# A global-filter token mixer and a hard-swish FFN on one core: the 3008-point Fourier transform factored as 47 x 64 in the other order, with token blocks cut across 94-token units

## The chip, the cores and the metric

One core of one Trainium2 chip. The metric is device microseconds of one execution. Runs of one kernel agree here within about 0.2%. A ratio is the mean time of one kernel's runs over that of the kernel before's runs of the same rounds on the same chip, so it is not quite the ratio of the medians that are quoted beside it.

## The reference

```python
# x: (8, 3008, 256); filt_r, filt_i: (1505, 256); w_in: (256, 2048); w_out: (2048, 256); x and filters float32, w_in and w_out float64
X = np.fft.rfft(x, axis=1)
Y = X * (filt_r + 1j * filt_i)[None, :, :]
y = np.fft.irfft(Y, n=3008, axis=1).reshape(8 * 3008, 256)
h = y @ w_in
out = (h * np.clip(h + 3.0, 0.0, 6.0) / 6.0) @ w_out          # (24064, 256)
```

## The kernel before

3008 = 47 x 64. Each batch's transform runs in two stages of dense matrices with a pass through memory between them, is multiplied by the filter, and comes back in two stages. In the kernel before, the first stage takes 64-point transforms over 47 residues (groups of four residues in two halves: 6 units a batch, four 64x64 matmuls of 512 columns each). The second stage has 32 matrices of 96 x 128, the inverse second stage 32 of 128 x 96; two matrices make a unit. The last inverse stage (`n_unit`) puts 4 x 128 tokens into a block of 512. The FFN takes 47 blocks in 8 steps each (376 steps), with Strassen products: 7 matmuls of 256 columns and 14 of 128 columns a step. Batch 0 is transformed ahead of the loop; batches 1 to 7 are transformed between the FFN steps of earlier batches.

```python
def b_unit(b, i):                                   # second stage, two matrices
    ...
    for u in range(2):
        nc.tensor.matmul(ps[:, u, :], st["tab", b, c][0][:, r + u, :],
                         st["t2", b, c][:, r + u, :], start=True, stop=True)

def bi_unit(b, i):                                  # its inverse
    ...
    for u in range(2):
        nc.tensor.matmul(ps[0:KR, u, :], st["tab", b, c][1][:, r + u, :], y[:, u, :], start=True, stop=True)

def n_unit(k, dh):                                  # last inverse stage: half of a block of 512 tokens
    ...
    for q in range(XC):                             # XC = 4
        nc.tensor.matmul(ps[:, ts(q, P)], st["t4", k][:, q, ts(dh, P)], wai, start=True, stop=True)

def out_5(k):                                       # the last sum of a block and its stores
    ...
    for q, n, _, ends in runs(k):
        for h, (b, n1) in enumerate(ends):
            nc.gpsimd.dma_start(rows[b, :, n1:n1 + n, :], o[h * 64:h * 64 + 64, q:q + n, :])

# ... batch 0, ahead of the loop; convert() makes float32 of one of 16 parts of the float64 FFN weights, on VectorE and GpSimd
for c in range(NB):                                 # NB = 6
    a_unit(0, c)
    z_store(0, c, nc.scalar)
    ...
    if c < 4:
        convert(1)
for i in range(K2 // 2 + 1):                        # 16 units of the second stage and its inverse
    ...
    if i % 4 == 2:
        convert(1)
```

In a matmul here the second operand is stationary (its weights are loaded) and the third is streamed. In `n_unit` the stationary operand is the data, 128 channels wide, and the streamed one is the table `wai`, one column a token.

## Time and profile before

| | before |
|---|---|
| median of the rounds shared with the changed kernel | 2854.55 us |
| span of the profiled run, mean granted clock | 2851.6 us, 0.986 |
| TensorE, VectorE, ScalarE, GpSimd busy | 96%, 74%, 47%, 18% |
| batch 0 done, loop begins (end of the first `psn` group on the chain) | 155.5 us |
| last matmul ends, span ends | 2842.1, 2851.6 us |

The stretches, and what binds each, are worked out in the prediction.

Names in the views: `psf` takes the results of the first, second and inverse second stage, `psn` those of the last inverse stage, `al` and `be` those of the FFN's up projection, `po` those of its down projection. An fp32 matmul stands in the trace as two records. The granted clock is the share of full speed that the throttle gave TensorE. "HWDGE" in the prediction means the DMAs that SP and ACT issue (the page calls their queues hardware_dynamic).

The end of the kernel before, in order of time (start, us, engine, line, operation):

```profile
2844.36 2.12 POOL L500 DMA_DIRECT2D out_dram<-o  x4 [0.51 <-POOL o L492]
```

Four stores, each from 64 partitions and 512 rows of output in all, are issued within 2.12 us, and 9.5 us after the last matmul the kernel is over.

### The profile page before, as it was taken

The numbers are of one execution on the slowest core, as the hardware profiler recorded it, in microseconds if no ns is written. First come the engines' busy times: TensorE is split into PE (matmuls) and PEld (weight loads), VectorE is DVE, ScalarE is ACT, GpSimd is POOL, SyncE is SP. The second block draws the span as 40 slices with busy tenths as digits, with TensorE's granted clock in tenths as the row PEclk, the third lists the DMA queues.
The fourth block names the chain that finished last, engine by engine and source line by source line (L and its number), as shares of the span: only waits on it lengthen the run. The fifth ranks groups of instructions, "written<-read, shape, count | busy, mean of one in ns | idle before, by whom it ended". The sixth has DMA issues, their size and how long they took to land.

```text
span 2851.6 us, 46327 instructions
## 1 busy us (share of the span) xinstructions
PE 2732.0 (96%) x17952; PEld 2469.6 (87%) x17952; DVE 2108.7 (74%) x3663; ACT 1326.1 (47%) x2622; POOL 520.3 (18%) x855
## 2 busy tenths in 40 slices
PE   3669999999999999999999999999999999999998
PEld 1347889999999999999999999999999999999998
DVE  4877877777767777777777777777777777766666
ACT  1124444544454445444544544454445444454544
POOL 2364221211121112111211121112110110010000
PEclk9779999999999999999999999999999999999999
DMA  7464533232222223222331332223221211010000
GB/s 190 137 162 132 152 107 90 72 86 78 71 78 81 79 72 84 70 78 79 87 96 47 93 85 64 83 60 95 77 63 54 71 51 54 17 51 16 23 8 16
DMA packets 104510, 221.66 MB, mean 78 GB/s; under 512 B 19936, under 2 KB 56932, under 8 KB 104292
## 3 DMA queue, kind: packets, MB, share of 16 engines
q1 hardware_dynamic: 69732, 127.97, 16.2%
q0 software_dynamic: 29056, 84.44, 10.5%
q10 hardware_dynamic: 5504, 6.30, 0.7%
q8 instruction: 142, 2.33, 0.4%
q14 instruction: 76, 0.62, 0.1%
HBM read 139.46 MB, written 79.17 MB: 77 GB/s over the span
## 4 chain that ended last, share of the span: by engine, by line
PE 91%; DVE 4%; DMA 3%; issue 1%; ACT 1%; SPq 0%; ACTq 0%; POOL 0%; POOLq 0%; DVEq 0%
PE po L465 40%; PE al L389 22%; PE be L389 17%; PE psf L301 4%; PE psf L329 4%; PE psn L374 3%; PE psf L275 2%; DMA z_tmp<-t 1%; DVE g L439 0%; DMA g_tmp<-t 0%; DVE s L315 0%; DVE s L314 0%; DMA ft<-in_filt_i_dram 0%; DMA ft<-in_filt_r_dram 0%; DVE rest L219 0%
## 5 line engine op out<-in xcount | busy, mean ns | idle before, releaser
L465 PEld LDWEIGHTS po<-w_out,g 128*128 128x128 f32 x10528 | 1409.6, 192 | 136.6 <-DVE g L439 25.0
L465 PE MATMUL po<-w_out,g 128*128 128x128 f32 x10528 | 1428.3, 276 | 24.3 <-DVE g L439 23.2
L434 ACT ACTIVATE r<-h,half_c 128x512 f32<-128x512 f32 x752 | 542.5, 721 | 331.6 <-DVE h L415 319.2
L389 PE MATMUL al<-xt,w_in 128*128 128x256 f32 x2256 | 676.7, 382 | 1.3 <-DVE h L420 0.8
L439 DVE SCALAR_TENSOR_TENSOR g<-r,h 128x512 f32<-128x512 f32 x752 | 517.5, 688 | 189.7 <-ACT r L434 173.7
L389 PE MATMUL be<-xn,w_in 128*128 128x256 f32 x1504 | 447.9, 379 | 0.0
L415 DVE TENSOR_TENSOR h<-be,s 128x512 f32<-128x512 f32 x376 | 259.8, 691 | 245.0 <-PE be L389 223.3
L389 PEld LDWEIGHTS al<-xt,w_in 128*128 128x128 f32 x2256 | 343.7, 193 | 3.3 <-issue 1.9
L429 ACT ACTIVATE h<-al 128x256 f32<-128x256 f32 x376 | 144.1, 383 | 383.6 <-PE al L389 383.6
L389 PEld LDWEIGHTS be<-xn,w_in 128*128 128x128 f32 x1504 | 286.0, 190 | 39.1 <-ACT xn L376 0.2
L420 DVE TENSOR_TENSOR h<-al,s 128x256 f32<-128x256 f32 x376 | 159.5, 424 | 199.5 <-PE al L389 199.4
L447 DVE TENSOR_TENSOR g<-g 128x512 f32<-128x512 f32 x376 | 261.6, 696 | 12.9
L410 ACT ACTIVATE s<-al 128x256 f32<-128x256 f32 x376 | 144.1, 383 | 222.3 <-PE al L389 222.3
L289 POOL DMA_DIRECT2D z_tmp<-t x336 | 166.5, 502 | 441.7 <-ACT t L278 426.3
L401 ACT ACTIVATE s<-be 128x256 f32<-128x256 f32 x376 | 144.1, 383 | 181.4 <-PE be L389 181.4
L389 PE MATMUL al<-xn,w_in 128*128 128x256 f32 x752 | 225.0, 381 | 0.5 <-ACT h L429 0.5
L389 PE MATMUL be<-xt,w_in 128*128 128x256 f32 x752 | 224.1, 380 | 0.0
L400 ACT ACTIVATE s<-al 128x256 f32<-128x256 f32 x376 | 144.1, 383 | 70.4 <-PE al L389 70.4
L449 DVE TENSOR_TENSOR g<-g 128x256 f32<-128x256 f32 x376 | 164.2, 437 | 12.8
L446 DVE TENSOR_TENSOR g<-g 128x256 f32<-128x256 f32 x376 | 164.1, 436 | 12.8
L301 PE MATMUL psf<-t,wb 96*128 96x256 f32 x512 | 143.2, 405 | 28.2 <-DMA t<-z_tmp 18.4
L382 POOL TENSOR_TENSOR xt<-xn 128x256 f32<-128x256 f32 x94 | 72.9, 776 | 521.0 <-ACT xn L376 520.9
(52 smaller groups left out, 2011.1 us busy)
## 6 DMA issues: line engine op xcount, KB each, us to landing
ft<-f_tmp SPq DMA_DIRECT2D x48, 512.0 KB
xc<-in_x_dram SPq DMA_DIRECT2D x88, 256.0 KB
z_tmp<-t POOLq DMA_DIRECT2D x336, 64.0 KB, 2.0
t<-z_tmp SPq DMA_DIRECT2D x56, 384.0 KB
g_tmp<-t POOLq DMA_DIRECT2D x56, 384.0 KB, 4.8
t<-g_tmp SPq DMA_DIRECT2D x160, 128.0 KB
out_dram<-o POOLq DMA_DIRECT2D x80, 256.0 KB, 3.7
wb<-wb_t SPq DMA_DIRECT2D x64, 192.0 KB
```

Source lines behind the costliest of these rows:

```text
L289: q.dma_start(z_d[b, :, r0 + h * H:r0 + h * H + 2, :], t[p0:p0 + 32, h, :, :])
L301: nc.tensor.matmul(ps[:, u, :], st["tab", b, c][0][:, r + u, :], st["t2", b, c][:, r + u, :], start=True, stop=True)
L389: nc.tensor.matmul(ps, w_in[p][:, w, :], x, start=start, stop=stop, skip_group_check=True)
L400: nc.scalar.activation(out=s[:, 0, :], in_=al, func=AXT.Copy)
L415: nc.vector.tensor_tensor(out=st["h"][0].rearrange("p (a n) -> p a n", a=2), in0=be, in1=s, op=ALU.add)
L420: nc.vector.tensor_tensor(out=st["h"][1][:, 256:512], in0=al, in1=s5, op=ALU.add)
L434: nc.scalar.activation(out=r, in_=st["h"][i], func=AXT.Relu, bias=half_c, scale=1.0 / 6.0)
L439: nc.vector.scalar_tensor_tensor(out=st["g", k, p][:, o:o + 2, :].rearrange("p a n -> p (a n)"), in0=st["r", i], scalar=1.0, in1=st["h"][i ...
L446: v.tensor_tensor(out=g[:, G1, :], in0=g[:, G3, :], in1=g[:, G22, :], op=ALU.add)
L447: v.tensor_tensor(out=g[:, G3:G2 + 1:2, :], in0=g[:, G3:G1 + 1, :], in1=g[:, G11:G11 + 1, :].broadcast_to([P, 2, 256]), op=ALU.subtract)
L449: v.tensor_tensor(out=g[:, G4, :], in0=g[:, G12, :], in1=g[:, G2, :], op=ALU.subtract)
L465: nc.tensor.matmul(st["po", k][bank][:, part, u, :], g[:, a, ts(u, P)], w_out[p][:, w, :], start=(p == 0 and n in OPENS and u == 0), stop= ...
```

## The change

The factors swap places. The 47-point stage comes first (with 24 of its 47 frequencies, as the input is real), in 8 units a batch in place of 6. The second stage then has 24 full matrices of 128 x 128 in place of 32 of 96 x 128, and so has its inverse. The last inverse stage gives units of 94 tokens, so that a block of 512 tokens is made of 6 or 7 pieces of units. The filter can be read straight from its tensor, and the stores move from GpSimd to SP, cut at unit and tile edges. The intent is a quarter less work in the second stages, on TensorE and on VectorE.

```diff
-N1 = 47        H = 24        K2 = 32        KR = 96      # (constants gathered on one line here)
+NA = 47        NC = 64       KH = 24        TOK = 94     # NB = 8 units, NU = 12 units of two matrices
...
-            nc.tensor.matmul(ps[0:KR, u, :], st["tab", b, c][1][:, r + u, :], y[:, u, :], start=True, stop=True)
+            nc.tensor.matmul(ps[:, u, :], st["tab", b, c][1][:, r + u, :], y[:, u, :], start=True, stop=True)
...
+    def pieces(k):
+        t = k * BLK
+        while t < (k + 1) * BLK:
+            u, r = divmod(t, TOK)
+            n = min(TOK - r, (k + 1) * BLK - t)
+            yield u // HC, u % HC, r, n, t - k * BLK
+            t += n
...
-        for q in range(XC):
-            nc.tensor.matmul(ps[:, ts(q, P)], st["t4", k][:, q, ts(dh, P)], wai, start=True, stop=True)
+        for i, (_, _, r, n, o) in enumerate(pieces(k)):
+            nc.tensor.matmul(ps[:, ds(o, n)], t4[k % 2][:, i, ts(dh, P)], wai[:, ds(r, n)], start=True, stop=True)
...
-        for q, n, _, ends in runs(k):
-            for h, (b, n1) in enumerate(ends):
-                nc.gpsimd.dma_start(rows[b, :, n1:n1 + n, :], o[h * 64:h * 64 + 64, q:q + n, :])
+        for b, j, r, n, t in pieces(k):
+            while n:
+                h, a = divmod(r, NA)
+                m = min(NA - a, n, P - t % P)
+                nc.sync.dma_start(raw(out, b * N + a * NC + h * HC + j, [[NC * D, m], [1, D]]),
+                                  o[t % P:t % P + m, t // P, :])
+                r, t, n = r + m, t + m, n - m
```

(Cut: the tables, the loads and stores between the stages, the places of the units among the FFN steps, and the scratch tiles of the weight conversions, which now share buffers with the filter units.)

More of the change, by code (lines that the diff above doesn't have):

```diff
@@ L21 @@
 N = 3008
-N1 = 47
-N2 = 64
+NA = 47
+NC = 64
+KH = 24
 NF = N // 2 + 1
@@ L28 @@
 DFF = 2048
-JT = DFF // P
-H = 24
-K2 = 32
-SL = 48
-KR = 2 * SL
 HALF = 64
+HC = NC // 2
 XC = 4
-NB = H // XC
+NB = HC // XC
 TC = 4
-NT = K2 // TC
+NT = KH // TC
+TB = 3
+NU = KH // 2
 NP = DFF // 256
-TB = 3
+TOK = 2 * NA
+BLK = 512
+NBLK = B * N // BLK
 def _make_tables():
-    n2 = np.arange(N2)
+    a = np.arange(NA)
+    c = np.arange(NC)
     wa = np.zeros((P, P))
-    wai = np.zeros((P, P))
+    wai = np.zeros((P, TOK))
     for h in range(2):
-        r = slice(h * 64, h * 64 + 64)
-        for k2 in range(K2):
-            th = 2 * np.pi * ((n2 * k2) % N2) / N2
-            c, s = np.cos(th), np.sin(th)
-            wa[r, k2] = wa[r, 64 + k2] = c
-            wai[h * 64 + k2, r] = c * (2.0 if k2 else 1.0)
-            if k2:
-                wa[r, 32 + k2] = wa[r, 96 + k2] = -s
-                wai[h * 64 + 32 + k2, r] = -2.0 * s
-            else:
-                alt = 1.0 - 2.0 * (n2 % 2)
-                wa[r, 32] = wa[r, 96] = alt
-                wai[h * 64 + 32, r] = alt
-    n1 = np.arange(N1)
-    wb = np.zeros((KR, K2, P))
-    wi = np.zeros((P, K2, KR))
-    re, im = slice(0, N1), slice(SL, SL + N1)
-    for k2 in range(K2):
-        for s in range(2 * H):
-            if s < H:
-                k, sign, q = k2 + 64 * s, 1.0, s
-            else:
-                j = s - H + 1
-                k, sign, q = 64 * j - (k2 if k2 else 32), -1.0, 32 + s - H
-                if j == H and k2:
-                    continue
-            th = 2 * np.pi * ((n1 * k) % N) / N
-            c, sn = np.cos(th), np.sin(th)
-            if k in (0, NF - 1):
-                sn = np.zeros(N1)
-            yr, yi = np.zeros(KR), np.zeros(KR)
-            if k2:
-                wb[re, k2, q] = c
-                wb[im, k2, q] = sign * sn
-                wb[re, k2, HALF + q] = -sn
-                wb[im, k2, HALF + q] = sign * c
-                yr[re], yr[im] = c, sign * sn
-                yi[re], yi[im] = -sn, sign * c
-            else:
-                rows = re if s < H else im
-                wb[rows, k2, q] = c
-                wb[rows, k2, HALF + q] = -sn
-                m = 1.0 if k in (0, NF - 1) else 2.0
-                yr[rows], yi[rows] = m * c, -m * sn
-            wi[q, k2], wi[HALF + q, k2] = yr, yi
@@ new lines, in _make_tables @@
+        for k in range(KH):
+            th = 2 * np.pi * ((a * k) % NA) / NA
+            for g in range(2):
+                wa[h * 64:h * 64 + NA, g * 64 + k] = np.cos(th)
+                wa[h * 64:h * 64 + NA, g * 64 + 32 + k] = -np.sin(th)
+            m = 2.0 if k else 1.0
+            wai[h * 64 + k, h * NA:(h + 1) * NA] = m * np.cos(th)
+            wai[h * 64 + 32 + k, h * NA:(h + 1) * NA] = -m * np.sin(th)
+    wb = np.zeros((P, KH, P))
+    wi = np.zeros((P, KH, P))
+    re, im = slice(0, NC), slice(NC, P)
@@ new lines, in _make_tables @@
+    for k in range(KH):
+        for q in range(64):
+            f, sign = (k + NA * q, 1.0) if q < 32 else (NA * (q - 31) - k, -1.0)
+            th = 2 * np.pi * ((c * f) % N) / N
+            cs, sn = np.cos(th), np.sin(th)
+            if f in (0, NF - 1):
+                sn = np.zeros(NC)
+            wb[re, k, q], wb[im, k, q] = cs, sign * sn
+            wb[re, k, HALF + q], wb[im, k, HALF + q] = -sn, sign * cs
+            wi[q, k, re], wi[q, k, im] = cs, sign * sn
+            wi[HALF + q, k, re], wi[HALF + q, k, im] = -sn, sign * cs
@@ L114 @@
     wi_d = nc.inline_tensor(wi_np, name="wi_t").ap()
-    z_d = nc.dram_tensor("z_tmp", (B, K2, KR, D), FP32, kind="Internal").ap()
-    g_d = nc.dram_tensor("g_tmp", (B, K2, KR, D), FP32, kind="Internal").ap()
-    f_d = nc.dram_tensor("f_tmp", (NT, P, TC, D), FP32, kind="Internal").ap()
+    z_d = nc.dram_tensor("z_tmp", (B, KH, P, D), FP32, kind="Internal").ap()
+    g_d = nc.dram_tensor("g_tmp", (B, KH, P, D), FP32, kind="Internal").ap()
     def pool(name, bufs, **kw):
@@ L124 @@
     const = pool("const", 1)
-    xp = pool("xp", 3)
     t1p = pool("t1p", 2)
@@ L131 @@
     t3p = pool("t3p", 2)
-    t4p = pool("t4p", 2)
     xnp = pool("xnp", 2)
@@ L138 @@
     op = pool("op", 2)
-    cv = pool("cv", 4)
     psF = pool("psF", 2, space=PSUM)
@@ L144 @@
     wa = const.tile([P, P], FP32, name="wa")
-    wai = const.tile([P, P], FP32, name="wai")
-    ft = [const.tile([P, TC, D], FP32, name="ft%d" % c) for c in range(TB)]
+    wai = const.tile([P, TOK], FP32, name="wai")
+    xs = [const.tile([P, XC, D], FP32, name="xs%d" % i) for i in range(3)]
+    ft = [const.tile([P, TC, D], FP32, name="ft%d" % i) for i in range(TB)]
+    t4 = [const.tile([P, 7, D], FP32, name="t4%d" % i) for i in range(2)]
     w_in = [const.tile([P, 7, P], FP32, name="w_in%d" % p) for p in range(NP)]
@@ L154, in raw, with table_load @@
         return bass.AP(tensor=src.tensor, offset=src.offset + row * D, ap=ap)
-    def f_load(b, c):
+    def table_load(b, c):
         t = ft[(b * NT + c) % TB]
-        if b > 1:
-            nc.sync.dma_start(t, f_d[c])
-            return
-        lo = 1 if c == 0 else 0
         for src, p0 in ((filt_r, 0), (filt_i, HALF)):
-            for r, n in ((0, 16), (16, H - 16)):
-                nc.sync.dma_start(t[p0 + r:p0 + r + n, :, :].rearrange("p a d -> p (a d)"),
-                                  raw(src, c * TC + 64 * r, [[64 * D, n], [1, TC * D]]))
-                if c == 0:
-                    nc.sync.dma_start(t[p0 + 32 + r:p0 + 32 + r + n, 0, :],
-                                      raw(src, 32 + 64 * r, [[64 * D, n], [1, D]]))
-                n = min(n, H - 1 - r)
-                nc.sync.dma_start(t[p0 + 32 + r:p0 + 32 + r + n, lo:TC, :],
-                                  raw(src, 64 + 64 * r - c * TC - lo, [[64 * D, n], [-D, TC - lo], [1, D]]))
-    def table_load(b, c):
-        f_load(b, c)
-        wb = tabp.tile([KR, TC, P], FP32, name="wb")
+            nc.sync.dma_start(t[p0:p0 + 32, :, :].rearrange("p k d -> p (k d)"),
+                              raw(src, c * TC, [[NA * D, 32], [1, TC * D]]))
+            nc.sync.dma_start(t[p0 + 32:p0 + 64, :, :], raw(src, NA - c * TC, [[NA * D, 32], [-D, TC], [1, D]]))
+        wb = tabp.tile([P, TC, P], FP32, name="wb")
         nc.sync.dma_start(wb, wb_d[:, ts(c, TC), :])
-        wi = tabp.tile([P, TC, KR], FP32, name="wi")
+        wi = tabp.tile([P, TC, P], FP32, name="wi")
         nc.sync.dma_start(wi, wi_d[:, ts(c, TC), :])
         st["tab", b, c] = wb, wi
-        if b == 1:
-            nc.gpsimd.dma_start(f_d[c], ft[(b * NT + c) % TB])
     NCONV = 16
@@ L213, in w_conv @@
         lo, hi = words[:, :, 0], words[:, :, 1]
-        big = cv.tile([P, 512], I32, name="big", tag="cv")
-        rest = cv.tile([P, 512], I32, name="rest", tag="cv")
+        big, rest = (sp.tile([P, 2, D], FP32, name=s).bitcast(I32).rearrange("p a n -> p (a n)")
+                     for s in ("s1", "s2"))
         v = nc.vector
@@ L256, in x_load @@
     def x_load(b, c):
-        t = xp.tile([P, XC, D], FP32, name="xc")
-        if c == NB - 1:
-            nc.vector.memset(t[64:P, XC - 1, :], 0.0)
-        rows = x[b].rearrange("(n2 n1) d -> n2 n1 d", n1=N1)
+        t = xs[(b * NB + c) % 3]
+        rows = x[b].rearrange("(a c) d -> a c d", c=NC)
         for h in range(2):
-            lo = h * H + c * XC
-            w = min(XC, N1 - lo)
-            nc.sync.dma_start(t[h * 64:h * 64 + 64, 0:w, :], rows[:, lo:lo + w, :])
-        st["x", b, c] = t
+            for r, n in ((0, 32), (32, NA - 32)):
+                nc.sync.dma_start(t[h * 64 + r:h * 64 + r + n, :, :], rows[r:r + n, ds(h * HC + c * XC, XC), :])
     def a_unit(b, c):
-        xc = st.pop(("x", b, c))
+        xc = xs[(b * NB + c) % 3]
         t = t1p.tile([P, 2, XC // 2, D], FP32, name="t1")
@@ L286, in z_store @@
                 p0 = g * 64 + ri * 32
-                r0 = ri * SL + c * XC + 2 * g
+                z = z_d[b, :, ts(ri, NC), :].rearrange("k (h j) d -> k h j d", h=2)
                 for h in range(2):
-                    q.dma_start(z_d[b, :, r0 + h * H:r0 + h * H + 2, :], t[p0:p0 + 32, h, :, :])
+                    q.dma_start(z[:, h, ds(c * XC + 2 * g, 2), :], t[p0:p0 + KH, h, :, :])
     def t2_load(b, c, q=None):
         q = q or nc.sync
-        t = t2p.tile([KR, TC, D], FP32, name="t2")
+        t = t2p.tile([P, TC, D], FP32, name="t2")
         q.dma_start(t, z_d[b, ts(c, TC), :, :].rearrange("k p d -> p k d"))
@@ L328, in bi_unit @@
         for u in range(2):
-            nc.tensor.matmul(ps[0:KR, u, :], st["tab", b, c][1][:, r + u, :], y[:, u, :], start=True, stop=True)
+            nc.tensor.matmul(ps[:, u, :], st["tab", b, c][1][:, r + u, :], y[:, u, :], start=True, stop=True)
         if r == 0:
-            st["t3", b, c] = t3p.tile([KR, TC, D], FP32, name="t3")
-        nc.scalar.activation(out=st["t3", b, c][:, r:r + 2, :], in_=ps[0:KR], func=AXT.Copy)
+            st["t3", b, c] = t3p.tile([P, TC, D], FP32, name="t3")
+        nc.scalar.activation(out=st["t3", b, c][:, r:r + 2, :], in_=ps, func=AXT.Copy)
     def g_store(b, c, q=None):
@@ L336, in g_store, with t4_load @@
         q.dma_start(g_d[b, ts(c, TC), :, :].rearrange("k p d -> p k d"), st.pop(("t3", b, c)))
-    def parts(k):
-        for q in range(XC):
-            v, j = divmod(XC * k + q, N1)
-            if j == N1 - 1:
-                yield q, 1, ((2 * v, H - 1), (2 * v + 1, H - 1))
-            else:
-                b, i = 2 * v + j // (H - 1), j % (H - 1)
-                yield q, 0, ((b, i), (b, H + i))
-    def runs(k):
-        found = []
-        for q, kind, ends in parts(k):
-            if found and not kind and not found[-1][2] and found[-1][3][0][0] == ends[0][0]:
-                found[-1][1] += 1
-            else:
-                found.append([q, 1, kind, ends])
-        return found
-    def t4_load(k):
-        t = t4p.tile([P, XC, D], FP32, name="t4")
-        for q, n, _, ends in runs(k):
-            for h, (b, n1) in enumerate(ends):
+    def pieces(k):
[5 more added lines that the diff above has]
+            t += n
+    def t4_load(k):
+        slot = 0
+        found = []
+        for b, j, _, _, _ in pieces(k):
+            if found and found[-1][0] == b:
+                found[-1][2] += 1
+            else:
+                found.append([b, j, 1])
+        for b, j, n in found:
+            for h in range(2):
                 for ri in range(2):
                     p0 = h * 64 + ri * 32
-                    nc.sync.dma_start(t[p0:p0 + 32, q:q + n, :],
-                                      g_d[b, :, ri * SL + n1:ri * SL + n1 + n, :])
-        st["t4", k] = t
+                    nc.sync.dma_start(t4[k % 2][p0:p0 + KH, slot:slot + n, :],
+                                      g_d[b, :, ds(ri * NC + h * HC + j, n), :])
+            slot += n
     def n_unit(k, dh):
@@ L372, in n_unit @@
         ps = psF.tile([P, 512], FP32, name="psn", tag="f")
-        for q in range(XC):
-            nc.tensor.matmul(ps[:, ts(q, P)], st["t4", k][:, q, ts(dh, P)], wai, start=True, stop=True)
+        for i, (_, _, r, n, o) in enumerate(pieces(k)):
+            nc.tensor.matmul(ps[:, ds(o, n)], t4[k % 2][:, i, ts(dh, P)], wai[:, ds(r, n)], start=True, stop=True)
         x = st["xn", k]
@@ L496, in out_5 @@
         o = st.pop(("o", k))[0].rearrange("p t u d -> p (t u) d")
-        rows = out.rearrange("(b n2 n1) d -> b n2 n1 d", n1=N1, n2=N2)
-        for q, n, _, ends in runs(k):
-            for h, (b, n1) in enumerate(ends):
-                nc.gpsimd.dma_start(rows[b, :, n1:n1 + n, :], o[h * 64:h * 64 + 64, q:q + n, :])
-    NBLK = B * N // 512
-    first = [(N1 * (b // 2) + (H - 1) * (b % 2)) // XC for b in range(B)]
+        for b, j, r, n, t in pieces(k):
[5 more added lines that the diff above has]
+                r, t, n = r + m, t + m, n - m
+    first = [b * N // BLK for b in range(B)]
     plan = {}
@@ L516 @@
         nc.vector.memset(half_c, 0.5)
+        for t in xs:
+            nc.gpsimd.memset(t, 0.0)
         nc.sync.dma_start(wa, wa_d)
@@ L521 @@
         w_load(1)
-        for t in ft:
-            nc.vector.memset(t, 0.0)
         done = 0
@@ L543 @@
         nc.sync.dma_start(wai, wai_d)
-        for i in range(K2 // 2 + 1):
-            if i < K2 // 2:
+        for t in t4:
+            nc.gpsimd.memset(t, 0.0)
+        for i in range(NU + 1):
+            if i < NU:
                 b_unit(0, i)
@@ L584, in places @@
             k = first[n]
-            u = [K2 // 2 - 1 - i for i in range(K2 // 2)]
+            u = [NU - 1 - i for i in range(NU)]
             b_at = [(k - 2 - j // 3) * NP + 6 - 2 * (j % 3) for j in u]
             bi_at = [i + 3 for i in b_at]
-            a_at = [(k - 13 + c) * NP for c in range(NB)]
+            a_at = [(k - 7 + c // 4) * NP + (0, 2, 5, 7)[c % 4] for c in range(NB)]
             if n == 1:
                 a_at = list(range(NB))
-                b_at = [8 + 3 * i // 2 for i in range(K2 // 2)]
-                bi_at = [10 + (3 * i + 1) // 2 for i in range(K2 // 2)]
-            elif n == 2:
-                a_at = [10 + 3 * c for c in range(NB)]
+                b_at = [10 + 7 * i // 4 for i in range(NU)]
+                bi_at = [i + 3 for i in b_at]
             return a_at, b_at, bi_at
@@ L605 @@
                 elif n > 1:
-                    at(max(prev[0][c + 3], s - 6), x_load, n, c)
+                    at(max(prev[0][c + NB - 3], s - 6), x_load, n, c)
             for c in range(NT):
-                s = bi_at[2 * (c - TB) + 1] if c >= TB else a_at[-1] + 2
+                s = bi_at[2 * (c - TB) + 1] if c >= TB else a_at[-1] + 1
                 if n > 1 and c < TB:
@@ L612 @@
                 at(s, t2_load, n, c)
-            for i in range(K2 // 2):
+            for i in range(NU):
                 at(b_at[i], b_unit, n, i)
```

## The prediction

> **What bounds the kernel now.** I read the page first, then the busy times by stretch, then the chain of waits. Section 1 of the page names the candidate:
>
> ```profile
> PE 2732.0 (96%) x17952; PEld 2469.6 (87%) x17952; DVE 2108.7 (74%) x3663; ACT 1326.1 (47%) x2622; POOL 520.3 (18%) x855
> ```
>
> A 96% average can hide stages, so I asked for four stretches (first the transform of batch 0, then the start of the block loop, the loop, the end; columns: PE, weight loads, DVE, ACT, POOL, clock, DMA share, GB/s):
>
> ```profile
> 0.00:155.00 155.00, 74.70 (x191) 38.83 (x192) 97.14 (x157) 17.87 (x30) 42.48 (x63) 0.86 0.61 166
> 155.00:240.00 85.00, 60.80 (x323) 46.77 (x323) 72.63 (x118) 27.46 (x55) 65.29 (x101) 0.84 0.48 123
> 240.00:2845.00 2605.00, 2596.47 (x17442) 2384.00 (x17440) 1938.97 (x3389) 1280.81 (x2537) 411.01 (x691) 1.00 0.25 71
> ```
>
> From 240 us on, TensorE is busy 2596.47 of 2605 us: it is the bound, and any matmul removed or added there moves the end. Before that it is not: 0 to 155 us goes through loads, the store of the first stage and VectorE. The chain of waits shows what each piece costs on the path in the loop (start, us, instructions; one fp32 matmul is two records):
>
> ```profile
> 1396.03 0.86 PE be L389 x4
> 1396.89 0.86 PE psf L301 x4
> ...
> 1403.04 0.86 PE be L389 x4
> 1403.90 0.86 PE psf L329 x4
> 1404.77 0.44 PE po L465 x4
> ...
> 1410.05 0.86 PE be L389 x4
> 1410.92 1.02 PE psf L275 x8
> 1411.94 0.64 PE po L465 x4
> ```
>
> The reader is to see: two second-stage matmuls of 256 columns take 0.86 us, so 0.43 each; a first-stage unit takes 1.02 and delays what follows by 0.64 - 0.45 = 0.19, so 1.21; two 128-column matmuls take 0.44, so 0.22 each. An FFN step alone takes 7.01 - 0.86 = 6.15 us.
>
> **What the Trainium skill says.** (1) "TensorE: Matmul & The Clock Gate", section "LDWEIGHTS (loading the stationary operand)": a load takes P/1.2 ns, P the columns of the stationary operand, 107 ns at 128, however few columns are streamed. The trace agrees in slope:
>
> ```profile
> L275 PEld LDWEIGHTS psf<-xc,wa 64*64 64x64 f32 x384 | 13.7, 141 | 52.9 <-ACT t L278 25.0 <-issue 18.0 <-DVE s L315 3.7
> L374 PEld LDWEIGHTS psn<-wai,t 128*128 128x128 f32 x752 | 100.1, 194 | 13.5 <-issue 8.8
> ```
>
> 64 columns more cost 194 - 141 = 53 ns (0.83 ns a column); the other 88 ns are latency, overlapped, since loads follow each other every 110 ns. (2) The same page, "Back-to-back issue gap": N/2.4 + 2.5 ns per pass when warm, and the spacing of a load-and-matmul stream is set by both. In an fp32 record two passes of 128 columns should take 106.7 ns plus about 5; 110 is measured, so a 128-column matmul already stands at its weight load. (3) "TensorEngine Tiling (Array Packing)", "Tiling Modes": 64x64 gives four independent tiles. Agrees: four 512-column matmuls in 1.02 us, where one alone would need 0.86. (4) "DMA: Bandwidth & Descriptors", section "Why a DMA increments its semaphore by 16 and not by 1": the number of engines is the largest divisor up to 16 of the slowest dimension, and on HWDGE the lowest-numbered engines. The kernel before stores 64 rows at a time, so no line of its trace tests this.
>
> **The change part by part.** Counts are of the two built programs.
>
> Second stage and its inverse: 256 + 256 matmuls become 192 + 192. An eighth belongs to batch 0, ahead of the loop. In the loop 448 become 336: -112 x 0.43 = **-48 us**. That the matrices grow from 96 to 128 rows costs nothing in streamed columns.
>
> First stage: 48 units become 64, in the loop 42 become 56: +14 x 1.21 = **+17 us**.
>
> Last inverse stage (psn): here the hidden cost lies. The moved columns stay at 48,128 in all, but a block of 512 tokens now takes 6 or 7 pieces of at most 94 columns in place of 4 of 128, so 376 matmuls become 604. A 94-column record streams 2 x 94/2.4 = 78 ns, less than its 107 ns weight load (the stationary side is the 128-column data tile). If the load sets the pace each piece costs the same 0.22 us as a full one: in the loop 592 - 368 = 224 more, **+49.5 us**. FFN products and sums are untouched. TensorE's sum in the loop: -48 + 17 + 49.5 = **+18 us**; the saving is paid back.
>
> VectorE: two matmuls share a unit of five operations of 0.69 us, and 128 units become 96: -110 us, of which 7/8 lie beside a full TensorE and count for nothing. In batch 0, VectorE does bind: the chain of waits puts four units and one weight conversion at about 20.7 us (81.9 to 102.6 to 123.3). Twelve units and three conversions in place of sixteen and four: **-21 us**. The conversion left over goes to the loop's start, where VectorE is the limit: +5 at most, I take +3.
>
> Start: eight first-stage units in place of six. A unit takes 6.6 us here, set by the store of z_tmp (evictions at 10.3, 17.6, 23.3, 29.6, 35.7, 43.2). The bytes are the same, but 64 DMAs go out in place of 48, from 24 rows. Between +0 and +13; I take **+8**. So the loop starts at about 155 - 13 = 142 us.
>
> End: the page shows stores that go out from GpSimd in pieces of 256 KB:
>
> ```profile
> out_dram<-o POOLq DMA_DIRECT2D x80, 256.0 KB, 3.7
> q10 hardware_dynamic: 5504, 6.30, 0.7%
> ```
>
> The new stores are 696 DMAs on SP, cut at 47-row and 128-row edges. Walking the pieces with rule (4), 18,376 of 24,064 rows fall to a single engine (47 rows: 1 engine), 356 to 435 in each block, 359 in the last. The ACT queue's packets, of 1.1 KB, took 0.7% x 16 x 2851.6 / 5504 = 58 ns each; so a block's store holds one engine for some 23 us of its 57 us, and the last one for 21. Before, TensorE ends at 2842.1 and the span 9.5 us later. After, I estimate 1.7 (last sums) + 1 + 21 + 2 = 26: **+16 us**.
>
> Sum: 2854 + 18 - 13 + 3 + 16 = 2878; plus 6 for new waits where batches meet (below): **2884 us**.
>
> **The rivals.**
> (a) The weight load does not set the pace of short matmuls. Then psn costs nothing more beyond a few ns a piece (some 228 x 15 = 3 us), TensorE's loop falls by about 28 us, and the time is near 2838. For it: loads can run ahead, and PEld is busy 87% with overlapping records. Against it: the slope above, and a load of 107 ns per 78 ns of streaming can't be hidden in a row of such pieces; only the first one of six or seven.
> (b) The queue of one DMA engine becomes a wait. With 23 us of stores and its 1/16 of the rest (183 MB/16 = 11.5 MB at some 58 ns a KB: 670 us in the span, 14 us a block), the engine is about 65% full: no bound by itself, but loads issued behind a block's store wait up to 23 us. Most loads are issued 7 to 10 steps of 6.15 us ahead. The tight ones are the first inverse load of each batch, issued three steps (18 us) before its use and two steps after a store burst, and the second stage's first load, now two to three steps behind the last first-stage unit. Seven such meetings of 0 to 7 us: 6 is my guess for the sum, 50 the worst. If a 1-row packet costs 120 ns in place of 58, the engine is overfull, and stores and loads drag the loop to 3000 or more.
> (c) GpSimd is freed of 112 stores and gains 112 of z_tmp: no change; at 18% busy it binds nothing.
> (d) The end's store is spread over all engines after all: then 16 us less, 2868.
>
> **Range and chances.** (a) at its fullest and a short end give 2825; the sum without guesses gives 2878; bad queueing at every meeting gives 2930. I hold the weight-load argument at 85%, and one-engine stores at 80%. Eight times in ten: 2848 to 2920. The edges of 2% are 2797 and 2911: below needs a gain that no part of the sum holds (0.04); above needs (b) to bite (0.18).
>
> **What would show it.** Right: the psn group has 1208 records, and seven pieces take 1.5 us on the chain of waits with records 110 ns apart even for 94 columns; second-stage groups have 384 records each at 0.43 us a matmul on the path; the loop begins near 142 us; TensorE still about full after 240 us; the span ends some 26 us after the last matmul. Wrong: psn pieces that follow at 80 ns a record (rival a); idle TensorE before psn or second-stage matmuls put down to a DMA (rival b); a tail under 15 us (d). What would upset the number most is a slow single-engine store, which I could not see in the trace before.

## The result, and the profile after

The changed kernel takes 2875.36 us (median of 4 runs, 2874.12 to 2877.08) against 2854.55; the ratio is 1.0072 (95% interval 1.0055 to 1.009). It computes the right result. By the 2% rule it is the same; it is slower by 0.7%, clear of noise. The prediction said 2884.

| | before | after | predicted |
|---|---|---|---|
| first second-stage matmul of batch 0 | 57.3 us | 61.2 us | +8 |
| from there to the first `psn` | 94.6 us | 74.5 us | -21 |
| loop begins | 155.5 us | 141.0 us | 142 |
| loop, to the last matmul | 2686.6 us | 2710.6 us (+24) | +27 (18 of work, 3, 6) |
| last matmul to end | 9.5 us | 20.7 us (+11) | +16 |

The page's first section, and the stretches of the changed kernel (columns as in the prediction):

```profile
PE 2745.6 (96%) x18280; PEld 2487.8 (87%) x18280; DVE 1991.8 (69%) x3492; ACT 1326.2 (46%) x2622; POOL 508.7 (18%) x836
```

```profile
0.00:141.00 141.00, 65.72 (x185) 33.07 (x186) 75.68 (x124) 17.73 (x30) 42.96 (x60) 0.86 0.60 182
141.00:230.00 89.00, 62.68 (x319) 46.84 (x319) 76.68 (x123) 26.50 (x53) 69.14 (x101) 0.84 0.39 110
...
500.00:1000.00 500.00, 500.00 (x3398) 459.87 (x3397) 352.97 (x621) 244.55 (x484) 79.88 (x138) 1.00 0.28 80
```

The table is of one profile of each kernel. Five other profiles of the changed kernel's start, from experiments below that alter nothing before the loop, have the first second-stage matmul at 62.9 to 66.4 us in place of 61.2; from there to the first `psn` they take 74.8 to 77.6 us, so their loop begins 2 to 7 us later. The first row is thus +4 here and +6 to +9 there; of the kernel before there is one profile.

VectorE lost 117 us of work, as meant, and TensorE stayed the bound: 500 of 500 us busy. So those 117 us bought time only ahead of the loop. The chain of waits of the changed kernel shows a half block's seven pieces, and the groups show what they are (out x in, count, then busy us and mean ns):

```profile
1417.21 0.86 PE be L341 x4
1418.08 1.48 PE psn L326 x14
1419.55 0.53 PE po L417 x4
```

```profile
L326 PEld LDWEIGHTS psn<-wai,t 128*128 128x128 f32 x1208 | 152.0, 194 | 15.3 <-issue 10.6
L326 PE MATMUL psn<-wai,t 128*128 128x94 f32 x840 | 115.0, 283 | 9.7 <-DMA t<-g_tmp 9.7
```

Seven matmuls of at most 94 columns take 1.48 us, and the pair after them 0.53 in place of 0.45: 1.56 / 7 = 0.223 us each, though 94 columns at the rate of a 256-column matmul (0.43 us) would stream in 0.158. Records of the down projection that have run tell how far each kernel is (x is their count; each step has 28). Before, then after:

```profile
0.00:500.00 500.00, 154.80 (x1092) 0.93 0.50 138
0.00:1000.00 1000.00, 420.32 (x3056) 0.96 0.39 108
...
0.00:2500.00 2500.00, 1223.85 (x9008) 0.99 0.31 86
```

```profile
0.00:500.00 500.00, 165.54 (x1160) 0.93 0.40 116
0.00:1000.00 1000.00, 431.60 (x3123) 0.97 0.34 98
...
0.00:2500.00 2500.00, 1227.12 (x8992) 0.99 0.29 83
```

At 500 us the changed kernel is 68 records ahead (17 us at some 4 records a us), at 1000 still 67, and at 2500 it is 16 behind. The shorter start is given back in the full loop. No wait takes part in that: of TensorE's waits from 230 us on the longest and the only one for a transfer are

```profile
PE po L417 <- DVE g L391: 1.5, 2, 0.9
...
PE psn L326 <- DMA t<-g_tmp: 0.4, 1, 0.4
```

(us in total, times, longest). Last, the end: the last sum and the stores in order of time, then three stretches after it (last column GB/s):

```profile
2852.90 0.43 DVE L447 TENSOR_TENSOR o<-po,o 128x256 f32<-128x256 f32 x1
2853.36 10.49 SPq L453 DMA_DIRECT2D out_dram<-o  x14
```

```profile
2858.00:2864.00 6.00, 0.00 (x0) 0.00 (x0) 0.00 (x0) 0.00 (x0) 0.00 (x0) 0.50 0.10 31
2864.00:2870.00 6.00, 0.00 (x0) 0.00 (x0) 0.00 (x0) 0.00 (x0) 0.00 (x0) 0.50 0.07 24
2870.00:2872.00 2.00, 0.00 (x0) 0.00 (x0) 0.00 (x0) 0.00 (x0) 0.00 (x0) 0.50 0.02 8
```

Fourteen stores are issued in 10.49 us, and for six more microseconds data goes out at 24 GB/s with a DMA share of 0.07, about 1 of 16 engines.

### The profile page after: what moved, and what is told of

Its sections match the earlier page's. It is cut to its first block, busy times and chain, and to the rows that moved or that the text cites. A ratio compares the mean times of both kernels' runs of the same rounds, so it can differ in the third digit from the quotient of the medians.

```text
span 2872.3 us, 47938 instructions
## 1 busy us (share of the span) xinstructions
PE 2745.6 (96%) x18280; PEld 2487.8 (87%) x18280; DVE 1991.8 (69%) x3492; ACT 1326.2 (46%) x2622; POOL 508.7 (18%) x836
## 4 chain that ended last, share of the span: by engine, by line
PE 90%; DVE 4%; DMA 3%; POOL 1%; issue 1%; SPq 1%; ACT 1%; ACTq 0%; POOLq 0%; DVEq 0%
PE po L417 40%; PE al L341 22%; PE be L341 16%; PE psn L326 4%; PE psf L257 3%; PE psf L285 3%; PE psf L231 2%; DMA z_tmp<-t 1%; SPq L453 0%; DVE g L391 0%; DVE s L271 0%; DMA out_dram<-o 0%; DVE s L270 0%; POOL z_tmp L245 0%; DMA bits<-in_moe_w_out_dram 0%
## 5 line engine op out<-in xcount | busy, mean ns | idle before, releaser
L245 POOL DMA_DIRECT2D z_tmp<-t x448 | 226.2, 513 | 375.5 <-ACT t L234 366.9
L326 PEld LDWEIGHTS psn<-wai,t 128*128 128x128 f32 x1208 | 152.0, 194 | 15.3 <-issue 10.6
L341 PEld LDWEIGHTS be<-xt,w_in 128*128 128x128 f32 x752 | 143.2, 190 | 19.4
```

Source lines behind the costliest of these rows:

```text
L245: q.dma_start(z[:, h, ds(c * XC + 2 * g, 2), :], t[p0:p0 + KH, h, :, :])
L326: nc.tensor.matmul(ps[:, ds(o, n)], t4[k % 2][:, i, ts(dh, P)], wai[:, ds(r, n)], start=True, stop=True)
L341: nc.tensor.matmul(ps, w_in[p][:, w, :], x, start=start, stop=stop, skip_group_check=True)
```

## The experiments

My theory: a short fp32 matmul costs its weight loads and not its columns, so the last inverse stage took back the second stages' saving; the start gained on VectorE; and the end waits for one DMA engine. The rivals are in the expectations. Each edit is made on the changed kernel unless it says otherwise.

**Every piece cut in two** (right result).

```diff
-            nc.tensor.matmul(ps[:, ds(o, n)], t4[k % 2][:, i, ts(dh, P)], wai[:, ds(r, n)], start=True, stop=True)
+            for r2, n2, o2 in ((r, n // 2, o), (r + n // 2, n - n // 2, o + n // 2)):
+                nc.tensor.matmul(ps[:, ds(o2, n2)], t4[k % 2][:, i, ts(dh, P)], wai[:, ds(r2, n2)], start=True, stop=True)
```

> The changed kernel with every piece of the last inverse stage cut in two: 1208 matmuls in place of 604, the same columns streamed, correct result. Theory (a short fp32 matmul costs its two weight loads, 0.22 us, whatever it streams): 592 more in the loop x 0.222 = +131 us, so about 3006 us, and the chain of waits shows 13 or so pieces in some 2.9 us with records 110 ns apart. Rival (cost follows the columns, plus a few ns a matmul): under +10 us, so about 2883.

Measured: 3026.8 us, ratio 1.0599 (1.0583 to 1.0615); about +151 us. The chain of waits of this run:

```profile
1430.98 2.60 PE psn L327 x24
1433.58 0.52 PE po L418 x4
```

Twelve matmuls of 47 columns and fewer take 2.60 + 0.07 us: 0.223 each, the same as at 94 columns. The rival is out by an order of size. Most of the 20 us above the expected 131 go with a lower clock: the mean granted clock was 0.978 over 3026.2 us against 0.985 over 2872.3, and scaled to full clock the two spans would differ by 2959.6 - 2829.2 = 130 us, a rough figure, as the start waits for transfers and VectorE. In the trace the clock falls to one half nine times between 416 and 2813 us, for 3.4 us each, which costs some 15 us; in the changed kernel it stays full from 213 to 2855 us. Whether the rows of short matmuls bring this on, no run tests.

**Four full matmuls in place of the pieces** (wrong result; every load kept).

```diff
-        for i, (_, _, r, n, o) in enumerate(pieces(k)):
-            nc.tensor.matmul(ps[:, ds(o, n)], t4[k % 2][:, i, ts(dh, P)], wai[:, ds(r, n)], start=True, stop=True)
+        for q in range(4):
+            nc.tensor.matmul(ps[:, ts(q, P)], t4[k % 2][:, q, ts(dh, P)], wai, start=True, stop=True)
```

(`wai` is widened to 128 columns.)

> The changed kernel with four 128-column matmuls for each half of a block in the last inverse stage, as the kernel before had, in place of six or seven pieces; wrong result on purpose (the columns belong to the wrong units), all loads kept. Same columns, 376 matmuls in place of 604. Theory (weight load sets the pace): 224 fewer in the loop x 0.222 = -50 us, about 2826 us. Rival (cost follows the columns): no change, 2872 to 2876.

Measured: 2827.02 us, ratio 0.9900 (0.9885 to 0.9915), against 1.0072 for the changed kernel: -0.0172 x 2855 = -49 us. Each ratio is known to some 4 to 5 us; the term of +49.5 us in the prediction agrees within that. Without it the change would have gained 1%.

**The same pieces, but each streams up to 128 columns** (what is too much is overwritten by the next piece).

```diff
-            nc.tensor.matmul(ps[:, ds(o, n)], t4[k % 2][:, i, ts(dh, P)], wai[:, ds(r, n)], start=True, stop=True)
+            w = min(P, BLK - o)
+            nc.tensor.matmul(ps[:, ds(o, w)], t4[k % 2][:, i, ts(dh, P)], wai[:, ds(r, w)], start=True, stop=True)
```

(`wai` is repeated to 256 columns.)

> The changed kernel with the pieces of the last inverse stage streaming up to 128 columns each (what is too much is overwritten by the next piece, so the result is right): 604 matmuls as before, 21,120 more columns streamed, which is 35 us[...]. Theory (up to 128 columns the weight load sets the pace): no change, within 3 us of 2875. Rival (cost follows the columns): +35 us, 2910.

Measured: 2874.95 us, ratio 1.0068 (1.0053 to 1.0083), no change. On the chain seven pieces still take what they took:

```profile
1420.83 1.48 PE psn L328 x14
1422.30 0.53 PE po L419 x4
```

21,120 more columns are free; at the 0.43 us of 256 columns they would be 35 us. With the two runs above: the cost goes with the count of matmuls at any width from some 40 to 128 columns.

One rival is left. In all these runs the stationary operand has 128 columns, so a fixed cost of some 110 ns a record that is not the weight load would give the same times. That it is the load is argued from the Trainium skill's 107 ns (in the prediction) beside the 110 ns measured; no run changes the width of the stationary operand or uses one load for several short matmuls.

**The second stage's matmuls run twice** for batches 1 to 7.

```diff
-            nc.tensor.matmul(ps[:, u, :], st["tab", b, c][0][:, r + u, :],
-                             st["t2", b, c][:, r + u, :], start=True, stop=True)
+            for _ in range(2 if b else 1):
+                nc.tensor.matmul(ps[:, u, :], st["tab", b, c][0][:, r + u, :],
+                                 st["t2", b, c][:, r + u, :], start=True, stop=True)
```

> The changed kernel with every matmul of the second stage run twice for batches 1 to 7 (the second writes the same values, the result is right): 168 more 256-column matmuls in the loop. Theory (each costs 0.432 us of a full TensorE, so the 112 that the change removed were worth 48 us): +72.5 us, 2948. Rival (part of them lay beside other waits): clearly less, +50 or below.

Measured: 2950.32 us, ratio 1.0334 (1.0316 to 1.0351): +0.0262 x 2855 = +75 us for 168 matmuls, 0.445 each. The saving of 112 was worth 48 to 50 us.

**The first stage's matmuls run twice** for batches 1 to 7.

```diff
-        for g in range(2):
+        for g in (0, 1, 0, 1) if b else (0, 1):
```

> The changed kernel with the four matmuls of every first-stage unit run twice for batches 1 to 7 (same values, right result): 56 more groups of four 64x64 matmuls of 512 columns in the loop. The path view gives 1.02 us for a group and 0.19 for the change to and from the small tiles, which the second group does not pay again. Theory (four tiles run at once and TensorE is full): 56 x 0.85 to 1.02 = +48 to +57 us, 2923 to 2932, so the 14 more units of the change cost some 17 us with their 0.19. Rival (the tiles run two at a time when repeated): +95 us or more.

Measured: 2919.67 us, ratio 1.0229 (1.0211 to 1.0246): +45 us, a little under the range. The chain shows a doubled group:

```profile
1483.63 1.88 PE psf L231 x16
1485.51 0.64 PE po L417 x4
```

The second group adds 1.88 - 1.02 = 0.86 us. That is 48 us over 56 units; the eight units of batch 1 run at the start of the loop, where TensorE is not full, which would account for the rest. The four small tiles do run at once.

**The stores back on GpSimd.**

```diff
-                nc.sync.dma_start(raw(out, b * N + a * NC + h * HC + j, [[NC * D, m], [1, D]]),
+                nc.gpsimd.dma_start(raw(out, b * N + a * NC + h * HC + j, [[NC * D, m], [1, D]]),
```

> The changed kernel with its 696 output stores issued by GpSimd, as the kernel before did with its 112, in place of SP. Theory (the end is 11 us longer because 14 stores take 10.5 us to issue on SP and then drain through one engine at 24 GB/s): from GpSimd they take about 14 x 0.54 = 7.5 us and are spread over more engines, so the time from the last matmul to the end falls from 20.7 to about 13 us: 2868. The loop stays as it is, as TensorE waits for none of this. Rival 1 (one engine in any case): no change, 2875. Rival 2 (GpSimd gets too busy, 508 to some 880 us, and delays the sums of the up projection): slower, 2885 or more, with TensorE idle before al or be matmuls.

Measured: 2876.27 us, ratio 1.0074 (1.0057 to 1.0091): no change, a miss. The stores did spread, and the data was out more than 8 us before the end (columns as in the prediction):

```profile
2860.00:2865.00 5.00, 0.00 (x0) 0.00 (x0) 0.00 (x0) 0.00 (x0) 3.08 (x7) 0.50 0.20 58
2865.00:2873.00 8.00, 0.00 (x0) 0.00 (x0) 0.00 (x0) 0.00 (x0) 0.00 (x0) 0.50 0.00 0
```

What the program then waits for stands in the trace among the bookkeeping instructions, which the views leave out. Each engine ends with a DRAIN and meets the others at a barrier. SP had seen the last store land and was there at 2865.1 us; GpSimd's DRAIN ran from 2861.6 to 2872.9 us, 11.3 us long. In the kernel before, whose last four stores GpSimd issued too, its DRAIN took 5.1 us and ended 1.7 us after SP was ready; with the stores on SP it is over at 2855.8, before the stores land. So the gain of spreading was there and was lost to GpSimd's DRAIN; why that is so long stays open. None of TensorE's waits in the loop (230 to 2840 us) is put down to GpSimd, so its added work delayed nothing there.

**The stores cut into groups of 16 rows and a rest.**

```diff
                 m = min(NA - a, n, P - t % P)
+                m = m // 16 * 16 or m
```

> The changed kernel with each output store cut into a part of whole 16-row groups and a rest under 16 rows (47 rows become 32 + 15), all on SP. Theory (rows of a 47-row store all go through one engine, which drains at 24 GB/s, so the last 359 rows take 15 us): the plateau of 24 GB/s at the end goes, and what is left is the issue of some 28 stores, at the 0.42 us median of such an issue in the loop 12 us, so the end comes 3 us earlier: 2872. Rival (an issue of a store costs 0.75 us, as 14 took 10.5 us, whatever its rows): 28 x 0.75 = 21 us, the end comes 3 to 5 us later: 2879. In the loop nothing changes in either.

Measured: 2869.68 us, ratio 1.0053 (1.0038 to 1.0068), 5.4 us less than the changed kernel by the ratios, where 3 were expected. The end in order of time, and a stretch of it:

```profile
2854.84 0.42 DVE L447 TENSOR_TENSOR o<-po,o 128x256 f32<-128x256 f32 x1
2855.29 10.52 SPq L454 DMA_DIRECT2D out_dram<-o  x26
```

```profile
2860.00:2866.00 6.00, 0.00 (x0) 0.00 (x0) 0.00 (x0) 0.00 (x0) 0.00 (x0) 0.50 0.17 47
```

Twenty-six stores are issued in the time that fourteen took, and the span ends 2.8 us after the last issue in place of 8.5, 15.0 us after the last matmul in place of 20.7. The plateau of 24 GB/s is gone. The rival of a fixed 0.75 us a store is out: an issue takes 0.27 to 0.42 us here, and took 0.26 to 1.93 us with uncut stores.

**The last block's stores issued by SP and ACT in turn, uncut.**

```diff
-                nc.sync.dma_start(
+                (nc.scalar if k == NBLK - 1 and i_dma % 2 else nc.sync).dma_start(
```

> The changed kernel with the 14 stores of the last block alone issued by SP and ACT in turn, unsplit. Theory (the one engine is what the end waits for, whichever queue feeds it): issuing is over some 5 us sooner, the plateau of 24 GB/s stays, the end moves by less than 2 us: 2874. Rival (the issue on SP sets the end): 5 us earlier, 2870.

Measured: 2875.57 us, ratio 1.0076 (1.0061 to 1.0091), no change. The two queues now take 8 to 9 us for seven stores each:

```profile
2853.78 8.29 SPq L455 DMA_DIRECT2D out_dram<-o  x7
2853.79 9.44 ACTq L455 DMA_DIRECT2D out_dram<-o  x7
```

All fourteen are issued in 9.4 us in place of 10.5; the 5 us sooner that I expected did not come. No single issue takes over 0.42 us here: the later ones wait for earlier stores. The program's stores share eight completion semaphores in turn, and a store that reuses one starts only when the one before it has landed: one of 47 rows lands at 2861.83 us, and the issue that waits for it starts at 2861.84. With one queue the same wait stands beside single issues of up to 1.93 us, which are gone when the stores are cut. Both fit waits for stores that one engine drains, and so the mean of 0.75 us. The theory of one engine stands.

**Eight weight conversions beside the first stage in place of four.**

```diff
-            if c < 4:
-                convert(1)
+            convert(1)
```

> The changed kernel with one weight conversion beside each of the eight first-stage units of batch 0 in place of the first four only, so 4 of 5.3 us fewer at the loop's start, where VectorE is busy 90% and TensorE waits for it. Theory (VectorE binds the second stage of batch 0 and the loop's start, and has nothing to do while the first stage waits for its stores): about -20 us, 2855; if the first stage is lengthened by the 2 MB of weights loaded earlier, up to 10 us of it comes back. Rival (the start is bound by transfers, and the conversions are hidden anyway): no change, 2875.

Measured: 2867.77 us, ratio 1.0048 (1.0033 to 1.0063): about -7 us, a third of what I expected. The chain of waits shows why (start, us):

```profile
17.92 5.33 DMA bits<-in_moe_w_in_dram
...
31.07 5.79 DMA bits<-in_moe_w_in_dram
...
46.00 7.47 DMA bits<-in_moe_w_in_dram
...
73.06 3.77 PE psf L257 x8
```

Two conversions take 13 to 15 us, as the load into one of two buffers waits for VectorE and GpSimd to be done with it; the second stage begins at 73.1 us in place of 61.2 (63 to 66 in most profiles). The loop then begins 12 us later and has four conversions fewer: from the first `po` matmul to the last it takes 2680.6 us in place of 2699.5, so a conversion at the loop's start costs 4.7 us.

**Six conversions beside the first stage, in the kernel before** (the same edit there, where the first stage has six units).

> The kernel before with one weight conversion beside each of its six first-stage units of batch 0 in place of the first four, so two of 5.3 us fewer at the loop's start. From the run with eight such conversions in the changed kernel: a pair of them takes 12 us there (load, VectorE, GpSimd, next load), and the first stage of the kernel before lasts 49 us, so three pairs fit without making it longer. Theory (VectorE binds the loop's start): -8 to -11 us, 2845, and the loop's first block no later. Rival (the first stage becomes as much longer): no change, 2855.

Measured: 2849.86 us over five rounds, ratio 0.9983 (0.9969 to 0.9996). About -5 us where -8 to -11 were expected. It is the only right version that stands below the kernel before, by 0.2%. The second stage of batch 0 began at 60.1 us in place of 57.3, so part of the gain may have gone into a longer first stage; one profile of each does not tell this from the spread of some 5 us that the changed kernel shows there. From the first `po` matmul to the last the loop takes 7.2 us less, 3.6 for each conversion.

**Six conversions and the cut stores, in the changed kernel.**

```diff
-            if c < 4:
+            if c < 6:
...
+                m = m // 16 * 16 or m
```

> The changed kernel with six conversions beside the first stage (not eight) and the stores cut into 16-row groups and a rest. If the two gains add: -5.5 for the stores, and for the conversions -8 (as with eight) to -11 (no longer first stage): 2856 to 2862. It would then stand level with or a little above the kernel before, as the 24 us that TensorE's loop has grown by stay. Rival (they overlap): 2866.

Measured: 2866.41 us, ratio 1.0040 (1.0027 to 1.0052): 9 us below the changed kernel, not the 13 to 19 expected. Against the cut stores alone the intervals overlap, so what six conversions add here is not told apart from little or nothing. It stays above the kernel before, as the two gains together are less than the loop's 24 us.

## Why the prediction was right

The time, 2875.4 us, lies in the range and 9 us under the point, and the class was the likeliest one.

- **The bound.** TensorE was full after 240 us before, and is after the change; its only wait for a transfer after 230 us is 0.4 us, which is what rival (b) would have lengthened.
- **Second stages, -48.** Confirmed by doubling: 0.445 us a matmul on the path, against 0.43 from the chain.
- **First stage, +17.** The doubled group cost 0.86 us on the chain; with its 1.02 and 0.19 the term was read rightly. Doubling measured 45 us where 56 x 0.86 = 48. The 0.19 stands on the chain alone.
- **Pieces, +49.5.** The decisive step, and the one with least to be seen in advance: nothing in the trace before ran fewer than 128 columns on a 128-column load. Three runs bear on it (+151, -49, 0), and rival (a), that width sets the cost, is out. What is shown is a fixed cost of 0.223 us a matmul; that the weight load is what fixes it is argued. So is the step from the page's gap formula, which is for one isolated matmul, to each pass of an fp32 record.
- **The sum of the loop.** Predicted +18 of work, and 3 + 6 for conversions and meetings of batches; measured +24. The meetings cost nothing (rival b did not bite in the loop). The conversion left over costs 3.6 to 4.7 us by the runs with more conversions up front, where 3 were taken. Some 2 us of the +24 are not assigned; runs of the changed kernel spread over 3 us. That 27 and 24 lie so near is in part luck: a term of 6 that was not there hid one that was taken too small and a rest.
- **The start, -13.** Measured -14.5 in the two profiles. The second stage of batch 0 gained 20 (predicted 21), read from the chain; no run tests it alone. The first stage cost 4, half of the 8 that I took from a range of 0 to 13, but 6 to 9 in five other profiles with the same code there, so 8 was no bad guess; `psn` cost 1.6 more, which I had left out.
- **The end, +16.** The mechanism was right (one engine), the size too large: a row took 1 KB / 24 GB/s = 43 ns, not 58, so the end grew by 11 us. By these profiles the point is high by 5 us at the end, 3 in the loop and 1.5 at the start.

## What to carry to other kernels

Count the matmuls of a stage as well as the columns: where the stationary operand changes each time, narrow pieces can cost as much as full ones (0.22 us each at 47 to 128 columns here, in fp32 with a 128-column stationary operand), and that took back all that a quarter less work in another stage had saved. Before celebrating work removed from an engine, look in which stretch that engine is waited for: 117 us of VectorE were worth about 20. Do not read a few us at the start from one profile: the same code began its second stage anywhere from 61 to 66 us. Choose row counts of stores that divide over many DMA engines, above all for the last ones, where nothing hides them.

## What the Trainium skill lacked or had wrong

- "TensorE: Matmul & The Clock Gate", "Back-to-back issue gap": the cycle table is for isolated matmuls, and for a stream of loads and matmuls the section has figures at 128 and 512 columns only. It lacks fp32 with a new 128-column stationary operand each time: measured 0.223 us a matmul, two records of 111 ns, at 47, 94 and 128 columns alike. The P/1.2 of "LDWEIGHTS (loading the stationary operand)" gives 107 ns and fits; that an fp32 matmul takes two such loads is not said on that page (604 psn matmuls have 1208 load records).
- "DMA: Bandwidth & Descriptors", "Why a DMA increments its semaphore by 16 and not by 1": the rule of the largest divisor agrees with the runs (47 rows: 24 GB/s at a DMA share of 0.07; 32 + 15 rows: no such plateau). It has no time for what this does to issuing: single issues of up to 1.93 us for uncut stores, at most 0.42 us for cut ones.
- No page was found that tells what stores from GpSimd add at the close of a program: its DRAIN took 11.3 us after fourteen stores in rows of 1 KB and 5.1 us after four larger ones, and the program ended within 1 us of it both times.
